# Block sums of the values from a copy of their own, and value tiles loaded in three pieces without the summary rows

## The chip, the core and the metric

The kernel runs on one core of a Trainium2 chip. The metric is the device time of one execution in microseconds (us); a figure for a kernel is the median of several executions. A profile is one more execution, recorded by the hardware; its span runs from the core's first instruction to its last. The engines are named TensorE (PE in rows, PEld its weight loads), VectorE (DVE), ScalarE (ACT), GpSimd (POOL) and SyncE (SP, which issues the DMA transfers).

## What is computed

Inputs are q, k and v of 4 batches, 8 heads, 768 positions and 64 columns, the routing matrix phi (512 x 32), and w1 and w2 of 8 experts. All is float32.

```python
k_sum = k.reshape(B, H, nb, block, D).max(axis=3)      # blocks of 32 positions, nb = 24
v_sum = v.reshape(B, H, nb, block, D).mean(axis=3)
scores_l = scale * q @ k.T      # kept where |i - j| < 16
scores_s = scale * q @ k_sum.T + log(block)
a = softmax(concatenate([scores_l masked, scores_s]))
x = a @ concatenate([v, v_sum])
# then a soft mixture of experts on x as (3072, 512):
logits = x @ phi
slots = softmax over rows(logits).T @ x       # 32 slots, 4 an expert
slot_out[e] = relu(slots[e] @ w1[e]) @ w2[e]
out = softmax over slots(logits) @ slot_out
```

So each query sees its 31 neighbours and 24 block summaries, and every block needs the maximum of its keys and the sum of its values.

## The kernel before, in words

**Tiles.** Work is cut into eight groups `hb` of four heads of one batch, and each group into three steps `tp` of 256 queries: 24 steps, `i` = 3 `hb` + `tp`. Within a step `tt` tells two halves of 128 queries, and `ab` two windows of 64 queries in each half. A window needs 96 positions (`W`) and 24 summaries (`NB`), together `U` = 120 rows. A value tile `v` is 128 partitions by 1040 columns: for both `ab`, both `tt` and four heads 64 columns and a one. It is laid out on the host; neighbouring windows overlap, so half of the positions stand there twice. Rows 96 to 119 of window `ab` = 0 and rows 32 to 55 of `ab` = 1 (`S0`) are left for the summaries; the load brings zeros and ones there, and `put_v` (L231) overwrites them.

**One step** (the loop at L522): `scores(i)` on TensorE (L253), `soft_max` (VectorE L271, GpSimd L275), `soft_exp` on ScalarE (L280), and for the step before, `j = i - 1`, transposes (`trans`, L286), their copies (`evac`, L291), `values` (L309) and a step later still `norm` (L329). TensorE's order is the order of the code.

**Summaries.** `k_max` (L184) takes block maxima of the next group's keys on VectorE in steps with `i % 3` = 1 and 2. `v_sum` (L200), called V(m) for group m, has four parts: 12 matmuls with an indicator matrix that add up blocks in the three value tiles of the group (L208); a copy on ScalarE and a difference on VectorE that split the sums into two parts (L219, L220), in a tile `vp`; two matmuls with a selection matrix (L224) that bring the 24 rows to their place; and a copy to `vsst` (L229). From there `put_v` writes them into the value tiles of the group. The four column groups of the array each take 32 output rows, so four of the 12 matmuls can run side by side.

**Where pieces stand.** `PLAN` (L42) lists for a step which parts of V, and of the routing (X a transposed x tile, L logits, t and D the slot sums), come where: text ahead of the bar before `soft_exp(i, 0)`, text behind it just before `values(j)`, the second string behind `values`. Each naming advances a piece by one part. V(m) begins in step 3m.

**Loads.** SyncE issues all loads in the order of the code: keys `k` (two of 472 KB a group), queries `q` (512 KB for two steps), value tiles (520 KB a step, requested four steps ahead into five buffers), and weights (512 KB each, 64 in all). `LOADS` (L39) says how many weights are requested at the end of each step; 36 in all, and 28 by the end of step 19. Eight semaphores take turns, so a load also waits until the one eight places before it has landed. A load into a buffer waits for the last reader of what was in it, and everything behind it on SyncE waits too.

**Behind the loop** come the last routing pieces (`TAIL`), a softmax over the slots, and the two expert stages with the rest of the weights (L651, L684) and the output (L711, L722).

Of the kernel before, what the change touches and what calls it, by code (L numbers as in the profile page):

```python
# [80 lines left out]
def attention_soft_moe(  # L81
# [48 lines left out]
    order = ["wa"] * NWA + "vp kp kp vp xs qp vp vp kp kp vp xs xs xs xs".split()  # L130
    NPRE = len(order)

    def load_piece():
# [4 lines left out]
        pool = {"wa": wa, "kp": kp, "qp": qp, "vp": vp_, "xs": xs}[slot[k]]
        t = pool.tile([128, 1024], F32, name=f"w{k}", tag=slot[k])
        p = pieces[k]  # L140
        if p[0] == "w1":
            _, e, c = p
            nc.sync.dma_start(out=t, in_=w1[e, 128 * c : 128 * c + 128, :])
        else:
            nc.sync.dma_start(out=t, in_=w2[p[1]])
# [19 lines left out]
    def load_v(i):  # L165
        if i < NSTEP:
            hb, tp = steps[i]
            v = vp_.tile([128, VC], F32, name=f"v{i}", tag="vp")
            nc.sync.dma_start(out=v, in_=vx[hb, tp])
# [30 lines left out]
    def v_sum(hb):  # L200
        pv = post_bank()
        for tp in range(TPS):
            v = vt[hb * TPS + tp]
            for tt in range(2):
                for ab in range(2):
                    g = tt * 2 + ab
                    ic = C_IND + 36 * ab + 4 - 2 * tp
                    nc.tensor.matmul(  # L208
                        pv[32 * g : 32 * g + 32, 0:256],
                        lhsT=cs[0:U, ic : ic + 32],  # L210
                        rhs=v[0:U, ab, tt, :, 0:64],
                        start=(tp == 0),
                        stop=(tp == TPS - 1),
                        tile_position=(0, 32 * g),
                    )
# [203 lines left out]
    def lanes():  # L419
# [317 lines left out]
def _layout(q, k, v):  # L737
# [22 lines left out]
    return kx.reshape(HB, 2, 128, KROW), np.ascontiguousarray(qx), vx.reshape(HB, TPS, 128, VC)  # L760


def _constants():
# [11 lines left out]
    ind = np.zeros((128, 2, 36), np.float32)  # L775
    for ab in range(2):
        for n in range(64):
            ind[16 + n + (NB if 16 + n >= S0[ab] else 0), ab, 4 + n // 32] = 1.0
    cst[:, C_IND : C_IND + 72] = ind.reshape(128, 72)
# [37 lines left out]
```

## Time and profile before

| | |
|---|---|
| median of three executions | 194.6 us (194.44 to 195.55) |
| the profiled execution | 193.69 us |
| its span | 191.9 us, granted TensorE clock 0.982 |
| TensorE busy | 170.6 us (89%) |
| VectorE, ScalarE, GpSimd busy | 114.7, 92.1, 78.7 us |
| bytes moved | 67.64 MB, mean 352 GB/s |
| first step's scores begin; step 21 begins | 7.96 us; 112.72 us |
| first expert matmul | 140.37 us |

A row of a timeline gives start, duration, engine, line, operation, what is written and read, a count, and in brackets how long the engine stood idle ahead of it and what ended that. A row of windows gives for a stretch the busy time of each engine, with the number of its instructions, the granted clock, the share of the transfer engines' time (it can pass 1 by a little) and what they moved. In rows of waits stand the total, the number and the longest.

### The profile page before, as it was taken

Reading aid. Unit: us, or ns where it says so; the run is one execution under the profiler, and the core shown is the slowest. Engines: PE = TensorE matmul, PEld = TensorE weight load, DVE = VectorE, ACT = ScalarE, POOL = GpSimd, SP = SyncE. Lnnn points to the kernel's source line nnn. Section 1 sums busy time; section 2 is a strip of 40 time slices with the busy share of each in tenths; the row PEclk is TensorE's granted clock in tenths of the full one; section 3 lists DMA queues with packets and bytes.
Section 4 is the critical chain, followed back from the end, with each engine's and each line's share of the span. In section 5 each row is a group of like instructions: output and inputs, shape, how many; then the busy total and the mean of one; then the engine's idle time right before and its main releaser. Section 6 shows DMA issues by size and latency. Waiting matters only on the chain.

```text
span 191.9 us, 7827 instructions
## 1 busy us (share of the span) xinstructions
PE 170.6 (89%) x3163; PEld 128.6 (67%) x3163; DVE 114.7 (60%) x580; ACT 92.1 (48%) x202; POOL 78.7 (41%) x106
## 2 busy tenths in 40 slices
PE   6979899799699999799999999998899998889950
PEld 5637678668567768578868786977456677667720
DVE  2539959649547967977967867755685020153460
ACT  2035656657464766756585484775222030033440
POOL 2047766666644685576684465780010000000000
PEclk9999999999999999999999999999969999999996
DMA  6999999999999899999999965967689999987696
GB/s 206 348 416 416 419 413 423 411 419 419 396 417 365 256 378 416 403 404 334 314 360 406 352 258 207 359 224 289 235 317 325 416 421 416 415 340 281 252 402 254
DMA packets 19331, 67.64 MB, mean 352 GB/s; under 512 B 2144, under 2 KB 2528, under 8 KB 19296
## 3 DMA queue, kind: packets, MB, share of 16 engines
q1 hardware_dynamic: 19296, 67.15, 90.2%
q8 instruction: 25, 0.41, 0.8%
q14 instruction: 10, 0.08, 0.1%
HBM read 60.85 MB, written 6.29 MB: 350 GB/s over the span
## 4 chain that ended last, share of the span: by engine, by line
PE 61%; DVE 14%; issue 7%; ACT 5%; DMA 4%; POOL 4%; SPq 2%; POOLq 0%; ACTq 0%; DVEq 0%
PE o L309 9%; PE hps L651 8%; PE so L684 8%; PE pt L286 7%; PE s L253 7%; PE pp L208 6%; DVE p L271 5%; DMA v<-vx 4%; PE op L711 4%; DVE kh L184 4%; POOL p L275 3%; PE pp L356 3%; PE pp L399 2%; PE pp L340 2%; DVE x L329 2%
## 5 line engine op out<-in xcount | busy, mean ns | idle before, releaser
L275 POOL TENSOR_TENSOR p<-p,m 128x480 f32<-128x480 f32 x48 | 46.4, 986 | 23.6 <-DVE m L271 23.3
L271 DVE CUSTOM_DVE_ANT_0 p<-s,cs 128x120 f32<-128x120 f32 x192 | 41.0, 278 | 5.7 <-PE s L253 4.7
L280 ACT ACTIVATE p<-p 128x480 f32<-128x480 f32 x48 | 29.0, 608 | 21.9 <-POOL p L275 21.6
L235 POOL COPY v<-vsst 24x520 f32<-24x520 f32 x47 | 29.1, 620 | 19.9 <-issue 17.6
L291 ACT COPY ptr<-pt 120x512 f32<-120x512 f32 x48 | 26.5, 588 | 21.3 <-PE pt L286 20.8
L309 PEld LDWEIGHTS o<-v,ptr 120*64 120x64 f32 x736 | 24.2, 137 | 10.0 <-issue 4.6
L309 PE MATMUL o<-v,ptr 120*64 120x65 f32 x736 | 27.7, 225 | 1.9 <-issue 1.5
L286 PE MATMUL pt<-ident,p 128*120 128x128 f32 x192 | 27.3, 281 | 0.8 <-ACT p L280 0.7
L253 PE MATMUL s<-k,q 64*64 64x120 f32 x768 | 26.2, 269 | 1.2 <-DVE m L271 0.6
L286 PEld LDWEIGHTS pt<-ident,p 128*120 128x120 f32 x192 | 20.4, 138 | 5.7 <-issue 2.8
L253 PEld LDWEIGHTS s<-k,q 64*64 64x64 f32 x768 | 20.4, 133 | 5.4 <-issue 2.5
L184 DVE TENSOR_REDUCE kh<-k 128x30 f32<-128x480 f32 (+1 forms) x32 | 16.1, 545 | 2.9 <-DMA k<-kx 2.9
L329 DVE TENSOR_TENSOR x<-o,z 128x512 f32<-128x512 f32 x23 | 15.9, 692 | 0.8
L271 DVE DVE_READ_ACCUMULATOR2_ANT m<- 128x1 f32 x192 | 16.0, 83 | 0.0
L651 PE MATMUL hps<-w,W1ST 128*32 128x256 f32 x256 | 15.7, 411 | 0.0
L720 DVE COPY ot<-op 128x512 f32<-128x512 f32 x12 | 7.9, 687 | 11.6 <-PE op L711 11.6
L684 PE MATMUL so<-w,W1ST 128*32 128x128 f32 x256 | 13.4, 275 | 0.9 <-issue 0.9
L208 PE MATMUL pp<-v,cs 120*32 120x256 f32 x192 | 12.4, 384 | 1.8 <-DMA v<-vx 1.0
L651 PEld LDWEIGHTS hps<-w,W1ST 128*32 128x32 f32 x256 | 8.9, 119 | 6.5 <-issue 1.8
L684 PE MATMUL so<-w,W2ST 128*32 128x128 f32 x256 | 13.1, 273 | 0.0
L340 PE MATMUL pp<-ident,x 128*128 128x128 f32 x88 | 12.5, 274 | 0.3 <-ACT xt L346 0.3
L346 ACT COPY xt<-pp 128x512 f32<-128x512 f32 x21 | 12.0, 602 | 0.1
(112 smaller groups left out, 180.2 us busy)
## 6 DMA issues: line engine op xcount, KB each, us to landing
w<-w SPq DMA_DIRECT2D x64, 512.0 KB, 8.1
v<-vx SPq DMA_DIRECT2D x24, 520.0 KB, 7.3
k<-kx SPq DMA_DIRECT2D x16, 472.0 KB, 7.2
q<-qx SPq DMA_DIRECT2D x12, 512.0 KB, 6.8
out<-ot SPq DMA_DIRECT2D x10, 512.0 KB, 3.6
out<-ot SPq DMA_DIRECT2D x4, 256.0 KB, 3.4
cs<-cst SPq DMA_DIRECT2D x1, 288.0 KB, 6.5
self__116<-selx SPq DMA_DIRECT2D x1, 64.0 KB, 6.2
```

The costliest lines, as they stand in the source:

```text
L184: nc.vector.reduce_max(out=kh[:, pr, :, n0 : n0 + m], in_=v[:, :, c0 : c0 + 16 * m].rearrange("p j (m k) -> p j m k", k=16), axis=AX,)
L208: nc.tensor.matmul(pv[32 * g : 32 * g + 32, 0:256], lhsT=cs[0:U, ic : ic + 32], rhs=v[0:U, ab, tt, :, 0:64], start=(tp == 0), stop=(tp == ...
L235: eng.tensor_copy(out=v, in_=src)
L253: nc.tensor.matmul(ps_[i, ab][h : h + 64, u, :], lhsT=qt[i // 2][rows, c : c + 64], rhs=kt[hb, pr][rows, k0 : k0 + U], start=True, stop=Tr ...
L271: nc.vector.tensor_tensor_reduce(out=p[:, n, :], in0=ps_[i, ab][:, 2 * tt + pr, :], in1=maskv[:, mk, :], scale=-0.125, scalar=-NEG, op0=AL ...
L275: nc.gpsimd.tensor_tensor(out=p, in0=p, in1=m.unsqueeze(2).broadcast_to([128, 4, U]), op=ALU.subtract)
L280: nc.scalar.activation(out=p, in_=p, func=AF.Exp, scale=-1.0)
L286: nc.tensor.transpose(pt[:, n, :], p[:, n, :], ident)
L291: nc.scalar.copy(out=ptr, in_=ptr_[i, tt])
L309: nc.tensor.matmul(o[64 * ab : 64 * ab + 64, h, :], lhsT=ptr[:, 2 * pr + ab, 64 * (r ^ ab) : 64 * (r ^ ab) + 64], rhs=v[0:U, ab, tt, h, :] ...
L651: nc.tensor.matmul(hps[32 * j : 32 * j + 32, :], lhsT=W1ST[:, c, 28 * e : 28 * e + 32], rhs=t[:, j, :], start=(k == 0), stop=(k == 31), ti ...
L684: nc.tensor.matmul(so[32 * j : 32 * j + 32, :], lhsT=W2ST[i][:, j, 28 * e : 28 * e + 32], rhs=t[:, i, j, :], start=(e == 0 and i == 0), st ...
```

## The change

`v_sum` reads an input of its own, `vox`: for each group all six tiles of 128 positions by four heads of 64 columns, each position once, 128 partitions by 1536 columns (768 KB). Six matmuls do what 12 did: tiles 0 to 3 in the four column groups, tiles 4 and 5 once more in the first two; the indicator and selection matrices change to match. `load_vo(hb)` requests it: group 0 right behind the selection matrix and ahead of the first value tiles, group 1 at the start as well (as two loads in two buffers of the pool for x tiles), and group m + 1 at the end of step 3m. The copy has a single buffer, `vo`, and V's split sums `vp` take the same buffer when the matmuls have read it.

A value tile is loaded in three pieces that leave out the rows for the summaries: rows 0 to 31 whole (4160 bytes each), rows 32 to 95 of the first half of the columns and rows 56 to 119 of the second half (2080 bytes each). The host packs the input to match (`_rows`). There are four value buffers, not five, and a tile is requested three steps ahead.

`PLAN` puts the first half of V(m) into step 3m - 1 for m from 1 on and the second half into step 3m (V7 has both in step 20), and shifts route pieces. `LOADS` asks for no weights in steps 0 to 2 and for more later. Two small tiles of the tail move to another buffer, since `vp` is no longer in their pool.

```diff
-LOADS = [1, 1, 1, 2, 2, 1, 2, 1, 2, 1, 1, 2, 2, 1, 1, 1, 1, 2, 1, 2, 3, 2, 2, 1]
+LOADS = [0, 0, 0, 1, 1, 2, 2, 1, 2, 1, 2, 2, 1, 2, 1, 2, 2, 2, 2, 2, 2, 3, 2, 1]
 PLAN = {
     0: ("V0 | V0", ""),
-    3: ("V1 | V1", "V1 V1"),
-    5: ("X0 X0 X1 X1", ""),
-    6: ("X2 X2 V2 | V2", "V2 V2"),
-    7: ("X3 X3", ""),
-    8: ("L0 | L0", ""),
-    9: ("t0 t0 X4 X4 V3 | V3", "V3 V3 D0 D0"),
+    2: ("V1 | V1", ""),
+    3: ("V1 V1", ""),
+    5: ("X0 X0 V2 | V2", ""),
+    6: ("V2 V2 X1 X1", ""),
+    7: ("X2 X2 X3 X3", ""),
+    8: ("L0 V3 | L0 V3", ""),
+    9: ("V3 V3 t0 t0", "D0 D0"),
...
-    20: ("X15 X15", "L3 L3"),
-    21: ("t3 t3 V7 | L3 V7 D3 D3", "V7 V7"),
-    22: ("X16 X16 X17 X17", ""),
+    20: ("X15 X15 V7 | V7", "V7 V7 L3 L3"),
+    21: ("t3 t3 X16 X16 | L3", "D3 D3"),
+    22: ("X17 X17", ""),
 }
-    vp_ = ctx.enter_context(tc.tile_pool(name="vp_", bufs=5))
+    vp_ = ctx.enter_context(tc.tile_pool(name="vp_", bufs=4))
+    vo = ctx.enter_context(tc.tile_pool(name="vo", bufs=1))
 def load_v(i):
-            nc.sync.dma_start(out=v, in_=vx[hb, tp])
+            n = S0[1]
+            nc.sync.dma_start(out=v[0:n], in_=vx[hb, tp, 0 : n * VC].rearrange("(p c) -> p c", p=n))
+            for ab in range(2):
+                p0, c0, o = (n, S0[1] + NB)[ab], VC // 2 * ab, n * VC + ab * 64 * VC // 2
+                nc.sync.dma_start(
+                    out=v[p0 : p0 + 64, c0 : c0 + VC // 2],
+                    in_=vx[hb, tp, o : o + 64 * VC // 2].rearrange("(p c) -> p c", p=64),
+                )
+    def load_vo(hb):
+        if hb == 1:
+            halves = [xs.tile([128, 1024], F32, name=f"vo1{n}", tag="xs")[:, 0:768] for n in range(2)]
+        elif hb < HB:
+            whole = vo.tile([128, 1536], F32, name=f"vo{hb}", tag="vo")
+            halves = [whole[:, 0:768], whole[:, 768:1536]]
+            nc.sync.dma_start(out=whole, in_=vox[hb])
...
 def v_sum(hb):
-        for tp in range(TPS):
-            v = vt[hb * TPS + tp]
-            for tt in range(2):
-                for ab in range(2):
-                    g = tt * 2 + ab
-                    ic = C_IND + 36 * ab + 4 - 2 * tp
-                    nc.tensor.matmul(
-                        pv[32 * g : 32 * g + 32, 0:256],
-                        lhsT=cs[0:U, ic : ic + 32],
-                        rhs=v[0:U, ab, tt, :, 0:64],
...
+        for t in range(6):
+            g = t % 4
+            ic = C_IND + 4 - 4 * (t // 4)
+            nc.tensor.matmul(
+                pv[32 * g : 32 * g + 32, 0:256],
+                lhsT=cs[:, ic : ic + 32],
+                rhs=kst["vo", hb][t],
+                start=(t < 4),
+                stop=(t + 4 > 5),
+                tile_position=(0, 32 * g),
+            )
-        vp = wk.tile([128, 2, 256], F32R, name="vp", bufs=1)
+        vp = vo.tile([128, 2, 256], F32R, name="vp", tag="vo")
 # start
-    for i in range(TPS):
-        load_v(i)
+    load_vo(0)
+    load_v(0)
+    load_v(1)
+    load_q(1)
+    load_k(1)
+    load_vo(1)
+    load_v(2)
+    load_v(3)
     nc.sync.dma_start(out=phi_sb.rearrange("p c s -> p (c s)"), in_=phi)
-    load_k(1)
-    load_q(1)
-    load_v(3)
-    load_v(4)
 # end of step i
+        if i > 0 and i % TPS == 0:
+            load_vo(i // TPS + 1)
         for _ in range(LOADS[i] if i < 20 else 0):
             load_piece()
         if i > 0:
-            load_v(i + 4)
+            load_v(i + 3)
```

The requests of SyncE at the start, behind the keys and queries of step 0; `self` is the selection matrix, and the numbers behind an underscore only tell buffers apart. Before:

```order
L506 DMA self__116<-selx 128x128
L169 DMA v_118<-vx 128x1040
L169 DMA v_120<-vx 128x1040
L169 DMA v_122<-vx 128x1040
L509 DMA phi_sb<-phi 128x128
L157 DMA k_125<-kx 128x944
L157 DMA k_127<-kx 128x944
L163 DMA q_129<-qx 128x1024
```

With the change:

```order
L527 DMA self__119<-selx 128x128
L189 DMA vo_121<-vox 128x1536
L173 DMA v_123<-vx 32x1040
L176 DMA v_123<-vx 64x520 x2
L173 DMA v_127<-vx 32x1040
L176 DMA v_127<-vx 64x520 x2
L166 DMA q_131<-qx 128x1024
L160 DMA k_133<-kx 128x944
L160 DMA k_135<-kx 128x944
L192 DMA vo_137<-vox 128x768
L192 DMA vo_138<-vox 128x768
```

V0 waited for the third value tile, and now waits for the first transfer behind the selection matrix; the next group's keys have the copy, two value tiles and q ahead of them.

TensorE at V7. Before, it stood in step 21, behind that step's scores (L253), transposes (L286) and the route piece t3 (L388):

```order
L286 MATMUL pt<-ident,p 120x128 x8
L388 MATMUL pp<-ident,dt 128x128
L208 MATMUL pp<-v_1875,cs 32x256 x4
L208 MATMUL pp<-v_1982,cs 32x256 x4
L208 MATMUL pp<-v_2086,cs 32x256 x4
L399 MATMUL pp<-x_1476,dsb 32x512 x2
L399 MATMUL pp<-x_1580,dsb 32x512 x2
L309 MATMUL o<-v_1764,ptr 64x65 x16
L224 MATMUL pp<-vp,sel 128x256 x2
```

With the change, in step 20, between the route transposes X15 (L361) and the values of step 19 (L330):

```order
L361 MATMUL pp<-ident,x_1591 128x128 x4
L229 MATMUL pp<-vo_2001,cs 32x256 x6
L330 MATMUL o<-v_1781,ptr 64x65 x16
L245 MATMUL pp<-vp,sel 128x256 x2
L377 MATMUL pp<-xt,phi_sb 32x128 x16
```

Twelve matmuls on three value tiles become six on one copy, and they stand one step earlier, ahead of the values of the step before.

The block sums' requests in the second half of the loop, from the end of step 17: the copy of group 7 stands behind the value tile of step 20 and ahead of step 18's weights.

```order
L160 DMA k_1896<-kx 128x944
L160 DMA k_1898<-kx 128x944
L146 DMA w_1900<-w 128x1024
L146 DMA w_1902<-w 128x1024
L173 DMA v_1904<-vx 32x1040
L176 DMA v_1904<-vx 64x520 x2
L189 DMA vo_2001<-vox 128x1536
L146 DMA w_2003<-w 128x1024
```

Before, V7 read the last of its three value tiles, which was requested at the end of step 19; its copy is now requested at the end of step 18.

More of the change, by code (lines that the diff above doesn't have):

```diff
@@ L35 @@
 C_N = 576
-LOADS = [1, 1, 1, 2, 2, 1, 2, 1, 2, 1, 1, 2, 2, 1, 1, 1, 1, 2, 1, 2, 3, 2, 2, 1]
+LOADS = [0, 0, 0, 1, 1, 2, 2, 1, 2, 1, 2, 2, 1, 2, 1, 2, 2, 2, 2, 2, 2, 3, 2, 1]
 PLAN = {
     0: ("V0 | V0", ""),
[19 rows of a table removed]
+    2: ("V1 | V1", ""),
[5 more added lines that the diff above has]
+    9: ("V3 V3 t0 t0", "D0 D0"),
+    10: ("X4 X4 X5 X5", ""),
+    11: ("X6 X6 V4 | V4", ""),
+    12: ("V4 V4 X7 X7", "L1 L1"),
+    13: ("t1 t1 X8 X8 | L1", ""),
+    14: ("D1 V5 | D1 V5", ""),
+    15: ("V5 V5 X9 X9", ""),
+    16: ("X10 X10 X11 X11", ""),
+    17: ("L2 V6 | L2 V6", ""),
+    18: ("V6 V6 t2 t2 | L2", "X12 X12 D2 D2"),
+    19: ("X13 X13 X14 X14", ""),
+    20: ("X15 X15 V7 | V7", "V7 V7 L3 L3"),
+    21: ("t3 t3 X16 X16 | L3", "D3 D3"),
+    22: ("X17 X17", ""),
     23: ("X18 X18", "x19 x19"),
@@ L86, in attention_soft_moe @@
     vx: bass.AP,
+    vox: bass.AP,
     phi: bass.AP,
@@ L128, in attention_soft_moe @@
     wt, slot = {}, {}
-    order = ["wa"] * NWA + "vp kp kp vp xs qp vp vp kp kp vp xs xs xs xs".split()
+    order = ["wa"] * NWA + "kp kp vp xs vo qp vp vp kp kp vp xs xs xs xs".split()
     NPRE = len(order)
@@ L137, in load_piece @@
         slot[k] = slot[k - NPRE] if k >= NPRE else order[k]
-        pool = {"wa": wa, "kp": kp, "qp": qp, "vp": vp_, "xs": xs}[slot[k]]
+        pool = {"wa": wa, "kp": kp, "qp": qp, "vp": vp_, "vo": vo, "xs": xs}[slot[k]]
         t = pool.tile([128, 1024], F32, name=f"w{k}", tag=slot[k])
@@ L168, in load_v @@
             v = vp_.tile([128, VC], F32, name=f"v{i}", tag="vp")
-            nc.sync.dma_start(out=v, in_=vx[hb, tp])
-            vt[i] = v.rearrange("p (a t h c) -> p a t h c", a=2, t=2, h=4)
+            n = S0[1]
[6 more added lines that the diff above has]
+                )
+            vt[i] = v.rearrange("p (a t h c) -> p a t h c", a=2, t=2, h=4)
+    def load_vo(hb):
[5 more added lines that the diff above has]
+            nc.sync.dma_start(out=whole, in_=vox[hb])
+        if hb == 1:
+            for n in range(2):
+                nc.sync.dma_start(out=halves[n], in_=vox[hb, :, 768 * n : 768 * n + 768])
+        if hb < HB:
+            kst["vo", hb] = [halves[t // 3][:, 256 * (t % 3) : 256 * (t % 3) + 256] for t in range(6)]
     kst = {}
@@ L423, in lanes @@
         yield
-        fg = wk.tile([1, 160], F32, name="fg", tag="vp", bufs=1)
+        fg = wk.tile([1, 160], F32, name="fg", tag="p", bufs=3)
         gm, f = fg[:, 128:160], fg[:, 0:128].rearrange("p (g s) -> p g s", g=4)
@@ L432, in lanes @@
         yield
-        R = wk.tile([128, 128], F32, name="R", tag="vp", bufs=1)
+        R = wk.tile([128, 128], F32, name="R", tag="p", bufs=3)
         nc.vector.tensor_scalar(out=R, in0=ps["stk"], scalar1=pc[:, 0:1], scalar2=None, op0=ALU.mult)
@@ L759, in _layout, with _rows @@
     qx = qx.reshape(HB * TPS // 2, 2, 128, 512).transpose(0, 2, 1, 3).reshape(HB * TPS // 2, 128, 1024)
-    return kx.reshape(HB, 2, 128, KROW), np.ascontiguousarray(qx), vx.reshape(HB, TPS, 128, VC)
+    return kx.reshape(HB, 2, 128, KROW), np.ascontiguousarray(qx), _rows(vx.reshape(HB, TPS, 128, 2, VC // 2))
+def _rows(vx):
+    n = S0[1]
+    parts = vx[:, :, :n], vx[:, :, n : n + 64, 0], vx[:, :, n + NB : n + NB + 64, 1]
+    return np.concatenate([p.reshape(HB, TPS, -1) for p in parts], axis=2)
 def _constants():
@@ L773, in _constants @@
     cst[:, C_MASK:C_IND] = mask.reshape(128, 4 * U)
[L775 to L779, printed above, removed]
+    cst[np.arange(128), C_IND + 4 + np.arange(128) // 32] = 1.0
     sel = np.zeros((128, 128), np.float32)
@@ L782, in _constants @@
         for n0 in VS:
-            sel[32 * (n // 2 % 4) + 2 * (n // 8) + n % 2, n0 + n] = 1.0
+            sel[32 * (n // 4 % 4) + 4 * (n // 16) + n % 4, n0 + n] = 1.0
     p = np.arange(128)
@@ L799 @@
         "vx": vx,
+        "vox": np.ascontiguousarray(
+            inputs["v"].reshape(HB, 4, 6, 128, D).transpose(0, 3, 2, 1, 4).reshape(HB, 128, 6 * 256)
+        ),
         "phi": np.ascontiguousarray(inputs["moe_phi"].reshape(4, 128, NS).transpose(1, 0, 2).reshape(128, 4 * NS)),
```

4 lines of the change are left out of this document (removed), and 9 rows, old and new, of the table PLAN.

## The prediction

> **What bounds the kernel now.** I read the page first: shares of the engines, then the chain of work that ended last.
>
> ```profile
> span 191.9 us, 7827 instructions
> PE 170.6 (89%) x3163; PEld 128.6 (67%) x3163; DVE 114.7 (60%) x580; ACT 92.1 (48%) x202; POOL 78.7 (41%) x106
> GB/s 206 348 416 416 419 413 423 411 419 419 396 417 365 256 378 416 403 404 334 314 360 406 352 258 207 359 224 289 235 317 325 416 421 416 415 340 281 252 402 254
> PE 61%; DVE 14%; issue 7%; ACT 5%; DMA 4%; POOL 4%; SPq 2%; POOLq 0%; ACTq 0%; DVEq 0%
> ```
>
> TensorE is the bound on average, but the transfers run close behind. So I cut the span into stages: up to the first work that needed summaries (13.3), two halves of the attention loop (to 112.7, where step 21 begins), its end with the routing, and the experts.
>
> ```profile
> core 0: us, PE busy (x) PEld busy (x) DVE busy (x) ACT busy (x) POOL busy (x), PEclk, DMA share, GB/s
> 0.00:13.30 13.30, 10.53 (x76) 6.93 (x76) 4.80 (x24) 1.89 (x2) 3.20 (x11) 1.00 0.84 315
> 13.30:62.40 49.10, 44.42 (x887) 35.19 (x887) 35.72 (x211) 29.84 (x64) 30.53 (x39) 1.00 1.02 410
> 62.40:112.70 50.30, 47.67 (x946) 37.53 (x937) 39.37 (x221) 33.37 (x76) 32.48 (x42) 1.00 0.96 357
> 112.70:140.30 27.60, 25.77 (x433) 19.59 (x432) 17.92 (x89) 15.09 (x39) 12.42 (x16) 1.00 0.73 268
> ```
>
> The reader is to see two things. In the loop TensorE is busy 44.42 of 49.10 us and 47.67 of 50.30: work taken off it is time gained. And the transfers are saturated (410 GB/s) in the first half, with little room in the second; a change that moves more bytes must be checked against that. Behind 112.7 there is room again (268 of 410 GB/s).
>
> **TensorE's part.** On the chain one V piece reads so (third column: what, with its count), with the step's scores and transposes before it:
>
> ```profile
> 83.02 0.98 PE s L253 x32
> 84.00 1.02 PE pt L286 x8
> 85.02 1.43 PE pp L208 x24
> 86.45 0.71 PE o L309 x19
> ```
>
> Each matmul gives two records, so 24 records are the 12 matmuls of a V piece: three rounds of four, one per column group of the array, 1.43 / 3 = 0.48 us a round. The new piece has six matmuls: a full round and one that uses two groups of four. If a half-filled round costs a full one, 0.95 us remain and 0.48 is saved; if time follows the number of matmuls, 0.72 is saved. I take 0.48, because the two matmuls of a group must follow each other. The seven pieces V1 to V7 lie in the TensorE-bound loop: 7 x 0.48 = **3.4 us** (at most 7 x 0.72 = 5.0). The contraction grows from 120 to 128 rows; the columns that stream through, 256, stay, so I count nothing for it. V0 is counted with the start.
>
> **The moved halves.** The first half of V(m) moves from step 3m to step 3m-1 and route pieces move the other way. Steps 2, 5, 8, ... are those in which VectorE also takes block maxima. These are seven of them, each from its first scores matmul to the next step's:
>
> ```profile
> 17.37:21.66 4.29, 3.47 (x74) 2.81 (x73) 4.12 (x24) 2.77 (x6) 2.96 (x4) 1.00 1.02 416
> 30.81:36.07 5.26, 4.29 (x84) 3.75 (x81) 3.88 (x23) 3.87 (x9) 3.65 (x5) 1.00 1.03 416
> 45.27:51.42 6.15, 4.39 (x108) 3.63 (x105) 4.31 (x24) 3.67 (x11) 4.43 (x6) 1.00 1.02 400
> 61.91:66.63 4.72, 4.35 (x85) 3.67 (x81) 4.62 (x25) 3.73 (x8) 3.11 (x5) 1.00 0.85 258
> 76.90:82.95 6.05, 5.02 (x93) 3.73 (x89) 5.14 (x25) 4.33 (x10) 3.90 (x6) 1.00 1.01 406
> 91.45:95.99 4.54, 4.37 (x109) 3.69 (x105) 4.38 (x25) 2.48 (x7) 2.93 (x5) 1.00 0.92 310
> 107.73:112.72 4.99, 4.99 (x112) 4.15 (x109) 3.25 (x21) 2.78 (x7) 2.19 (x4) 1.00 0.83 319
> sum 36.00, PE 30.87 PEld 25.43 DVE 29.71 ACT 23.64 POOL 23.16; mean PE 4.41 PEld 3.63 DVE 4.24 ACT 3.38 POOL 3.31
> ```
>
> TensorE idles 36.00 - 30.87 = 5.1 us there, and VectorE is nearly full in the first, fourth and sixth. Work put into these steps can lie beside what already makes TensorE wait. At worst nothing is hidden (0), at best all 5.1. I take **1.5 us**: some of the idle time stands behind the V piece's new place and isn't reached by it.
>
> **The start.** V0 now needs the first three value tiles. The rows are the arrival of the selection matrix, the last round of V0, the scores of step 1, and the first block maxima of the next keys:
>
> ```profile
> 8.85 0.29 POOL L517 CAST sel<-self__116 128x128 fp32r<-128x128 f32 x1 [7.26 <-DMA self__116<-selx]
> 12.75 0.16 PEld L208 LDWEIGHTS pp<-v,cs 120*32 120x32 f32 x8 [1.18 <-DMA v<-vx]
> 13.32 0.43 PE L253 MATMUL s<-k,q 64*64 64x120 f32 x8
> 16.61 1.57 DVE L184 TENSOR_REDUCE kh<-k 128x30 f32<-128x480 f32 x3
> ```
>
> Right behind the selection matrix the new order requests the copy, 786 KB, which at 410 GB/s lands at 8.8 + 1.9 = 10.7; six matmuls of 0.95 end at 11.6, and the scores of step 1 begin 1.7 us earlier. But then come v0, v1, q1 (0.97, 0.97 and 1.28 us at that rate) and both halves of the next keys (2.36): 16.3, where the maxima, 1.7 us earlier, would want them whole by about 16.0. V1's copy, two loads of 393 KB, lands at 18.2, wanted when step 2's transposes are done: 17.37 - 1.7 + 2.0 = 17.7. I count **1.0 us** of gain; the bounds are 0.4 (1.3 us of it are lost again) and 1.7.
>
> **Bytes.** The copy is 8 x 786 KB = 6.29 MB more. A value tile without the 24 overwritten rows of each half is 399 instead of 532 KB: 24 x 133 = 3.19 MB less. Net 3.1 MB more, 7.6 us at 410 GB/s, all before step 21. Is it in the way? The copy for V(m) must land before TensorE reaches V(m). I add the bytes requested ahead of it in the new order (keys, queries, values, copies, weights), take the first 13.3 us at 315 GB/s (4.19 MB) and the rest at 410, and set against it the place where V(m) would stand at today's pace (step's start, 2.0 us for scores and transposes, and the route pieces ahead):
> - V2: 10.2 MB, 27.9 us; place 33.2
> - V3: 15.7 MB, 41.5; place 48.3
> - V5: 28.5 MB, 72.5; place 80.0
> - V7: 41.2 MB, 103.5; place 110.2
>
> So the queue allows a gain of 5.3 us early and 6.6 late. The last place is read here (scores, transposes, route transposes, and the values matmuls ahead of which V7 will stand):
>
> ```profile
> 107.73 1.05 PE L253 MATMUL s<-k,q 64*64 64x120 f32 x32
> 108.71 1.09 PE L286 MATMUL pt<-ident,p 128*120 128x128 f32 x8
> 109.63 0.60 PE L340 MATMUL pp<-ident,x 128*128 128x128 f32 x4
> 110.16 1.35 PE L309 MATMUL o<-v,ptr 120*64 120x65 f32 x32
> ```
>
> Fewer weights in steps 0 to 4 make the early room; 28 pieces are requested by the end of step 19 in both, and what follows has the room behind 112.7, so the experts' stage is counted unchanged.
>
> **Requests.** SyncE issues three loads a value tile instead of one, 57 requests more in all (48 and nine for the copies).
>
> ```profile
> 3.06 1.56 SPq L169 DMA_DIRECT2D v<-vx  x3
> SPq L169 <- PE o L309: 48.8, 18, 4.7
> SPq L145 <- DMA w<-w: 10.4, 11, 2.0
> w<-w SPq DMA_DIRECT2D x64, 512.0 KB, 8.1
> v<-vx SPq DMA_DIRECT2D x24, 520.0 KB, 7.3
> ```
>
> One issue costs 1.56 / 3 = 0.52 us, so 30 us of SyncE; it waits 48.8 us for the values matmuls to release value buffers, which covers this. Two costs stay. A load waits until the one eight places before it has landed (the third row is such a wait): eight loads with six small ones among them hold 1.8 MB rather than 4.1, so the queue can run dry. And the copy shares its buffer with V's intermediate, so its request waits for V(m-1)'s second matmul, two steps (about 9 us at the new pace) before its use, while loads take 7 to 8 us to land; behind this wait stand the weights and the next value tile, which has three more steps. Bounds for both: nothing, as the landing times fit, and 4 us, half a microsecond or so at each V piece. I take **0.9 us** lost, mostly at V1 and V2.
>
> **Sum.** 1.0 + 3.4 + 1.5 - 0.9 = 5.0 us less. The profiled execution took 193.7 (span 191.9 and 1.8 around it); the median shown is 194.6. So 194.6 - 5.0 = **189.6 us**, own range 187 to 192.5 from the terms' bounds.
>
> **Rivals.** *Pieces of a tile move slowly (slower).* Every load of the trace fills all 128 partitions; the new value loads fill 32 or 64. No row prices that. If the first and the last piece (133 KB each, 0.32 us at 410 GB/s) run at half the rate, a tile costs 0.65 us more, 21 tiles by V7 13.7: its copy lands at 117.2, 7.0 behind today's place; with the 0.5 us that V7 itself saves, 6.5 slower: 201. It decides from about 0.31 us a tile, that is when three pieces take as long as the whole tile does today (1.30 us): then the 6.6 us of room are gone. Against it: two pieces of different rows may be in flight at once and share. The lower bound of this cost is nothing.
> [...]
>
> *VectorE keeps the step (no change).* In three of the seven steps VectorE was busy 4.1 of 4.3, 4.6 of 4.7 and 4.4 of 4.5 us. If its chain of scores, maxima and normalisation sets every step, TensorE's savings become idle time and only the start's 1.0 remains: 193.6. Against it: TensorE is the fuller engine in both halves of the loop.
>
> *The copy isn't early (no change).* Should the request wait for the second matmul cost each of V2 to V7 0.8 us, 4.8 are lost and the gain is gone: 194.4. For it: loads land 7 to 8 us after issue in a window of 9; against it: the queue holds fewer bytes now, so they land sooner.
>
> **How the numbers follow.** The forecast gets 0.62 (with 0.05 for a gain over 7.6 us, where idle time is filled better), no change through VectorE 0.10, through late copies 0.08, slow pieces 0.20. One per cent, 1.9 us, is about what a measurement here can tell from none (three runs spread by 1.1). So faster 0.62, same 0.18, slower 0.20. The range runs from 187.0, where all but the largest gains lie, over the no-change cases to 197.0, which takes in slow pieces up to a third of the loss worked out.
>
> **What would show it.** Right: V pieces of 12 records near 0.95 us, none preceded by a wait for the copy over half a microsecond, step 20 starting about 4 us earlier, idle time of steps 2, 5, 8 smaller. Wrong: value loads whose packets keep the transfer engines longer than their bytes ask for, or waits of TensorE for `vo` that grow from V3 to V7: then the slow pieces hold. Steps unchanged with more idle TensorE: VectorE.

## The result, and the profile after

The changed kernel takes 218.3 us (median of four executions, 216.54 to 223.65), the kernel before 194.7 on the same chip: a ratio of 1.123 [1.116, 1.130], 12% slower, where 189.6 us was forecast. (Medians are of all executions of a kernel, but ratios leave out those more than 1.5% above its fastest; the experiment `mid` below has for that reason one execution left and no interval.)

These are rows of the page of the kernel after: span, engines, bandwidth by slices, packets, and the shares of the chain of work that ended last.

```profile
span 215.2 us, 7788 instructions
PE 174.6 (81%) x3067; PEld 132.3 (61%) x3067; DVE 114.5 (53%) x580; ACT 92.6 (43%) x202; POOL 78.6 (37%) x106
...
GB/s 205 353 314 322 225 296 361 279 400 338 308 308 317 351 302 401 322 329 300 312 375 294 370 303 325 304 263 400 386 191 354 244 405 416 419 415 404 338 293 302
DMA packets 22163, 70.73 MB, mean 329 GB/s; under 512 B 3056, under 2 KB 3440, under 8 KB 22128
...
PE 52%; DMA 34%; issue 3%; SPq 3%; DVE 2%; POOL 1%; ACT 1%; POOLq 0%; ACTq 0%
```

The chain has turned from 4% DMA to 34%. The bytes are what was planned (70.73 MB, 3.09 more than before), but the slices in the first three quarters read about 320 GB/s; before, the first half of the loop read 410 and the second 357. The last quarter, which loads weights and no values, again has slices over 400.

The same stages as before, by windows of the kernel after (step 1 begins at 12.47, step 21 at 137.75):

```profile
0.00:12.47 12.47, 9.69 (x64) 6.92 (x64) 4.81 (x24) 1.89 (x2) 3.20 (x11) 1.00 0.85 275
12.47:66.39 53.92, 45.98 (x832) 36.91 (x830) 35.93 (x210) 29.73 (x64) 30.46 (x39) 0.87 1.02 321
66.39:137.75 71.36, 52.04 (x934) 40.78 (x931) 39.48 (x222) 34.77 (x78) 33.60 (x43) 0.90 1.03 328
137.75:163.60 25.85, 23.48 (x404) 17.92 (x400) 16.78 (x84) 14.27 (x36) 10.42 (x13) 1.00 0.91 316
163.60:215.20 51.60, 43.46 (x847) 29.79 (x846) 17.55 (x41) 11.95 (x23) 0.95 (x1) 0.94 0.91 357
```

In the loop the transfer engines are busy all the time (1.02 and 1.03), yet move 321 and 328 GB/s. So the queue did not run dry; each byte took longer. Step 21 starts 25.0 us later than before, the first expert matmul also 25.0 later (165.37 against 140.37), and the span ends 23.3 later: the whole loss is made in the loop.

Within the loop it sits in one kind of step, the seven with V(1) to V(7) (steps 2, 5, ... 20, the same class as in the prediction). Three of them and the sum, by windows of the kernel after:

```profile
46.43:57.27 10.84, 6.87 (x120) 4.96 (x116) 4.65 (x25) 4.35 (x12) 4.63 (x7) 0.74 1.04 327
103.78:113.29 9.51, 5.38 (x120) 4.05 (x116) 5.24 (x27) 4.53 (x13) 4.61 (x7) 1.00 1.03 337
123.42:137.75 14.33, 8.23 (x125) 6.07 (x123) 5.25 (x25) 4.52 (x10) 4.32 (x6) 0.76 1.03 317
...
sum 67.27, PE 42.79 PEld 30.38 DVE 34.99 ACT 30.17 POOL 32.43; mean PE 6.11 PEld 4.34 DVE 5.00 ACT 4.31 POOL 4.63
```

They took 36.00 us before and take 67.27 now: 31.3 us more, against a loss of 25.0 by step 21; the other steps got shorter. What TensorE waits for there stands in the waits of the kernel after:

```profile
PE pp L229 <- DMA vo<-vox: 23.7, 9, 6.1
```

and, in TensorE's timeline of step 20, where:

```profile
123.42 1.05 PE L274 MATMUL s<-k,q 64*64 64x120 f32 x32
124.41 1.09 PE L307 MATMUL pt<-ident,p 128*120 128x128 f32 x8
125.33 0.60 PE L361 MATMUL pp<-ident,x 128*128 128x128 f32 x4
132.03 1.92 PE L229 MATMUL pp<-vo,cs 128*32 128x256 f32 x12 [6.10 <-DMA vo<-vox]
133.88 2.00 PE L330 MATMUL o<-v,ptr 120*64 120x65 f32 x32
```

TensorE is done with scores and transposes at 125.9 and stands 6.1 us before V(7), whose copy is missing. The chain of the kernel after has these copies as its links (start, duration; here V2, V3, V5 and V7):

```profile
29.40 7.20 DMA vo<-vox
...
45.22 8.13 DMA vo<-vox
...
83.04 9.18 DMA vo<-vox
...
122.66 9.24 DMA vo<-vox
```

They land at 36.6, 53.4, 92.2 and 131.9; the prediction had them at 27.9, 41.5, 72.5 and 103.5. The error (8.7, 11.9, 19.7 and 28.4 us) grows with the number of value tiles moved, as it must if every tile costs too much. The waits themselves don't grow steadily: 0.77 us at V2, 3.97 at V3, 1.79 at V5 and 6.10 at V7.

**Theories.** *Rows* (A in the expectations): a load that fills only 32 or 64 neighbouring partitions is slow, so the three pieces of a value tile are. *Number of loads* (B): three small loads are slower than one whatever they fill, through SyncE's issues or the queue. *Bytes* (C): the copies' 6.3 MB are simply too many. Most of the experiments vary one of these at a time.

### The profile page after: what moved, and what is told of

It reads as the page before. It is cut to its first block, busy times and chain, and to the rows that moved or that the text cites. A ratio compares the mean times of both kernels' runs of the same rounds, so it can differ in the third digit from the quotient of the medians.

```text
span 215.2 us, 7788 instructions
## 1 busy us (share of the span) xinstructions
PE 174.6 (81%) x3067; PEld 132.3 (61%) x3067; DVE 114.5 (53%) x580; ACT 92.6 (43%) x202; POOL 78.6 (37%) x106
## 2 busy tenths in 40 slices
DMA packets 22163, 70.73 MB, mean 329 GB/s; under 512 B 3056, under 2 KB 3440, under 8 KB 22128
## 4 chain that ended last, share of the span: by engine, by line
PE 52%; DMA 34%; issue 3%; SPq 3%; DVE 2%; POOL 1%; ACT 1%; POOLq 0%; ACTq 0%
DMA vo<-vox 24%; PE o L330 8%; PE so L709 7%; PE hps L676 7%; PE s L274 6%; PE pt L307 6%; PE pp L229 4%; DMA v<-vx 4%; PE op L736 4%; DMA q<-qx 3%; DMA k<-kx 3%; PE pp L361 3%; PE pp L377 2%; PE pp L420 1%; SPq L173 1%
## 5 line engine op out<-in xcount | busy, mean ns | idle before, releaser
L330 PEld LDWEIGHTS o<-v,ptr 120*64 120x64 f32 x736 | 27.5, 153 | 10.5 <-issue 9.5
L330 PE MATMUL o<-v,ptr 120*64 120x65 f32 x736 | 31.2, 241 | 2.8 <-issue 2.4
L229 PE MATMUL pp<-vo,cs 128*32 128x256 f32 x96 | 11.8, 496 | 23.7 <-DMA vo<-vox 23.7
L274 PE MATMUL s<-k,q 64*64 64x120 f32 x768 | 28.2, 284 | 2.2 <-issue 1.8
L274 PEld LDWEIGHTS s<-k,q 64*64 64x64 f32 x768 | 22.0, 143 | 8.0 <-issue 5.8
L307 PEld LDWEIGHTS pt<-ident,p 128*120 128x120 f32 x192 | 20.9, 140 | 4.1 <-issue 3.0
L229 PEld LDWEIGHTS pp<-vo,cs 128*32 128x32 f32 x96 | 4.1, 127 | 28.7 <-issue 23.8
L241 DVE TENSOR_TENSOR vp<-pp,vp 128x256 fp32r<-128x256 f32 x8 | 3.4, 425 | 25.8 <-ACT vp L240 25.8
L676 PE MATMUL hps<-w,W1ST 128*32 128x256 f32 x256 | 15.2, 401 | 0.0
L709 PE MATMUL so<-w,W1ST 128*32 128x128 f32 x256 | 14.0, 275 | 1.2 <-issue 1.2
L361 PE MATMUL pp<-ident,x 128*128 128x128 f32 x88 | 12.9, 275 | 1.2 <-issue 0.9
```

Source lines behind the costliest of these rows:

```text
L229: nc.tensor.matmul(pv[32 * g : 32 * g + 32, 0:256], lhsT=cs[:, ic : ic + 32], rhs=kst["vo", hb][t], start=(t < 4), stop=(t + 4 > 5), tile_ ...
L274: nc.tensor.matmul(ps_[i, ab][h : h + 64, u, :], lhsT=qt[i // 2][rows, c : c + 64], rhs=kt[hb, pr][rows, k0 : k0 + U], start=True, stop=Tr ...
L307: nc.tensor.transpose(pt[:, n, :], p[:, n, :], ident)
L330: nc.tensor.matmul(o[64 * ab : 64 * ab + 64, h, :], lhsT=ptr[:, 2 * pr + ab, 64 * (r ^ ab) : 64 * (r ^ ab) + 64], rhs=v[0:U, ab, tt, h, :] ...
L361: nc.tensor.transpose(pv[:, 128 * c : 128 * c + 128], x, ident)
L676: nc.tensor.matmul(hps[32 * j : 32 * j + 32, :], lhsT=W1ST[:, c, 28 * e : 28 * e + 32], rhs=t[:, j, :], start=(k == 0), stop=(k == 31), ti ...
```

## Experiments

To compare transfer rates I use one window for all kernels, from 20 to 100 us, inside the loop. Its rows for the kernel before, and then for the kernel after:

```profile
20.00:100.00 80.00, 73.55 (x1461) 58.21 (x1461) 60.55 (x359) 51.42 (x115) 52.25 (x66) 1.00 0.99 385
```

```profile
20.00:100.00 80.00, 65.24 (x1168) 51.95 (x1172) 50.88 (x298) 42.48 (x93) 44.23 (x56) 0.87 1.02 321
```

385 GB/s before, 321 after, at a share of 0.99 and 1.02.

### 1. rows4, spread4, cols4: four loads a tile, cut in three ways

The kernel before, with each whole value tile loaded by four loads of 133 KB: 32 neighbouring partitions each, or every fourth partition, or 260 of 1040 columns of all partitions.

```diff
-            nc.sync.dma_start(out=v, in_=vx[hb, tp])
+            for n in range(4):
# rows4
+                nc.sync.dma_start(out=v[32 * n : 32 * n + 32], in_=vx[hb, tp, 32 * n : 32 * n + 32])
# spread4
+                nc.sync.dma_start(out=v[n:128:4], in_=vx[hb, tp, n:128:4])
# cols4
+                nc.sync.dma_start(out=v[:, 260 * n : 260 * n + 260], in_=vx[hb, tp, :, 260 * n : 260 * n + 260])
```

> The kernel before, with each value tile loaded as four loads of 32 neighbouring rows (133 KB each, 4160 bytes a row) in place of one; same bytes, nothing else changed. Theory A (a load that fills part of the partitions runs slowly, by which rows it fills): at half rate a tile costs 1.3 us more, 24 tiles 31 us; the loop's queue has some 7 us of room, so 212 to 222 us. Theory B (it is the number of loads and their size): slower too, and as much as the two kernels that cut the tile in another way. Theory C (only the copy's bytes slowed the changed kernel): within 1% of 194.7.

> The kernel before, with each value tile loaded as four loads of 32 rows again, but every fourth row (n, n + 4, n + 8, ...), so that each load is spread over all partitions; same bytes, same number and size of loads as with neighbouring rows. Theory A: 194 to 198 us, since each load reaches everything a whole tile reaches. Theory B: as slow as with neighbouring rows. Theory C: within 1% of 194.7.

> The kernel before, with each value tile loaded as four loads of 260 columns by all 128 rows (133 KB each, 1040 bytes a row). Theory A: 194 to 199 us, a little for shorter rows. Theory B: the slowest of the three, as its rows are shortest. Theory C: within 1% of 194.7.

| | us | ratio to before | GB/s, 20 to 100 us | transfer share |
|---|---|---|---|---|
| rows4 | 237.5 | 1.217 [1.205, 1.228] | 274 | 1.01 |
| spread4 | 204.1 | 1.049 [1.040, 1.058] | 360 | 0.99 |
| cols4 | 199.3 | 1.023 [1.016, 1.030] | 372 | 1.01 |

Same bytes, same number of loads, same load size: rows4 loses 22%, the others 5% and 2%. So neighbouring rows are what costs. Rows4 and spread4 lie well above what *Rows* expected (212 to 222 and 194 to 198 us), cols4 just above (194 to 199). The cut into more loads costs something too: with 72 loads more cols4 loses 4.5 us and spread4 9.6, some 0.06 and 0.13 us each (cols4 also has shorter rows, 1040 bytes for 4160). Why every fourth row is dearer than columns wasn't resolved.

### 2. halves and mid: fewer loads, other rows

Again the kernel before; `halves` has only 24 loads more than it, `mid` has 48.

```diff
-            nc.sync.dma_start(out=v, in_=vx[hb, tp])
# halves
+            for n in range(2):
+                nc.sync.dma_start(out=v[64 * n : 64 * n + 64], in_=vx[hb, tp, 64 * n : 64 * n + 64])
# mid
+            for n in (slice(0, 32), slice(32, 96), slice(96, 128)):
+                nc.sync.dma_start(out=v[n], in_=vx[hb, tp, n])
```

> The kernel before, with each value tile as two loads of 64 neighbouring rows (266 KB each). If it counts which rows a load fills, and rows 0 to 63 are served no better than 0 to 31: as slow as four loads of 32 neighbouring rows, 228 to 240 us. If a load of 64 rows has three quarters of the rate or so, 205 to 215. If it is the number of loads (24 more): 196 to 200.

> The kernel before, with each value tile as three loads of rows 0 to 31, 32 to 95 and 96 to 127 (133, 266 and 133 KB). If it counts which rows a load fills and the middle one, half of it in each half of the partitions, is served like a whole tile, half of the loss with four loads of 32 rows stays (237.5 - 194.9 = 42.6): 212 to 219 us. If any load of neighbouring rows below 128 is slow: 230 to 238. If it is the number of loads: 198 to 203.

`halves` took 241.1 us (240.1 to 245.61), 1.242 [1.230, 1.254], just above the 228 to 240 expected if rows count. The four executions of `mid` took 213.28, 217.32, 219.83 and 220.25 us, 1.10 to 1.13 times the kernel before; its profile is of the one at 219.83. The common window of halves, and then of mid:

```profile
20.00:100.00 80.00, 59.57 (x1038) 46.12 (x1041) 42.87 (x249) 36.17 (x80) 37.24 (x47) 0.86 1.03 277
```

```profile
20.00:100.00 80.00, 68.17 (x1245) 52.68 (x1244) 53.07 (x303) 44.18 (x95) 45.20 (x57) 0.94 1.03 318
```

Two loads a tile, of 64 rows each, are as slow as four of 32 (277 and 274 GB/s), so the number of loads falls as the main cause. With three loads, whose middle one takes rows 32 to 95, about half of the loss goes away (18.7 to 25.6 us of halves' 46.5 stay, by the fastest and the slowest execution): it matters which 64 rows. The reads from device memory are contiguous in rows4, halves and mid alike, so that side doesn't tell them apart. The transfer engines' share stays at 1.03. What makes rows 32 to 95 cheaper than rows 0 to 63 or 64 to 127 isn't shown by these runs.

The size is another matter. An estimate: in this window of halves, 23 loads of 266 KB are 6.1 of 22.1 MB, so values are 28% of the bytes. If all other loads ran at the 416 GB/s that `whole` (below) reaches, 1/277 = 0.72/416 + 0.28/x gives x = 149 GB/s for the halves, about a third of those 416 and not the half that the prediction's rival took. Part of that may be that other loads in the queue wait behind the slow ones; the runs don't separate it.

### 3. whole: the change with whole value tiles

The kernel after in all but the value loads: each tile is one load of 128 rows, the overwritten rows included, 3.2 MB more.

```diff
-            n = S0[1]
-            nc.sync.dma_start(out=v[0:n], in_=vx[hb, tp, 0 : n * VC].rearrange("(p c) -> p c", p=n))
...
+            nc.sync.dma_start(out=v, in_=vx[hb, tp])
```

> The changed kernel with one thing undone: a value tile is one load of 128 rows again (532 KB, with the rows that the summaries overwrite). 3.2 MB more are moved than in the changed kernel. Theory A: the queue moves 410 GB/s again, V7's copy lands near 111 us, and the time falls to 193 to 199 us. Theory B: likewise faster, by the 48 loads fewer. Theory C: slower than the changed kernel, 3.2 MB at its 325 GB/s being 10 us: 225 us or more.

It took 194.5 us, a ratio of 1.000 [0.995, 1.005] (the profiled execution 196.6). The pieces cost 218.3 - 194.5 = 23.8 us, net of the 3.2 MB that they save: the whole loss. The common window of whole:

```profile
20.00:100.00 80.00, 70.15 (x1389) 56.53 (x1387) 58.91 (x351) 50.37 (x111) 51.10 (x65) 0.98 1.02 416
```

The rate is 416 GB/s, nothing left. But the forecast gain doesn't appear either, and the waits and the last copy of whole (from its chain) say why:

```profile
PE pp L222 <- DMA vo<-vox: 13.1, 7, 3.8
```

```profile
101.26 11.31 DMA vo<-vox
```

V(7)'s copy lands at 112.6. The prediction's way of adding bytes, with 24 rows of each half put back in (44.0 MB ahead of it), gives 13.3 + (44.0 - 4.19) / 0.410 = 110.4, against a place of 110.2. So at full rate that method holds to 2.2 us, and it says that whole tiles and the copies together use up all the room.

### 4. thirds: the pieces' bytes and number, on all rows

The kernel after with three loads a tile of 260 columns by 128 partitions: 399 KB in three loads, as in the change.

```diff
+            for n in range(3):
+                nc.sync.dma_start(out=v[:, 260 * n : 260 * n + 260], in_=vx[hb, tp, :, 260 * n : 260 * n + 260])
...
-                    rhs=v[0:U, ab, tt, h, :],
+                    rhs=v[0:U, ab, tt * (1 - ab), h, :],
```

> The changed kernel with a value tile's three loads cut by columns instead of rows: 260 columns by all 128 rows each, 399 KB in sum as in the changed kernel, the same number of loads in the same places. The last quarter of a tile isn't loaded, and the values matmuls that need it take the quarter before; so those outputs are left out, at the same work. Theory A (which rows a load fills): the cost of the pieces goes, V7's copy lands near 104 to 108 us and the time is 188 to 195. Theory B (three small loads a tile are slow however cut): 214 to 221, as the changed kernel.

It took 195.6 us, 1.003 [0.998, 1.008], just above the 188 to 195 that *Rows* expected. The common window of thirds:

```profile
20.00:100.00 80.00, 71.07 (x1389) 57.94 (x1387) 59.11 (x346) 49.26 (x109) 50.50 (x64) 0.98 1.02 387
```

Bytes (70.73 MB), number of loads and order are those of the change; only the rows that a load fills differ (and with them the length of a row, 1040 bytes for 4160 and 2080), and 22.7 of the 23.6 us are gone. This is the cleanest proof of *Rows*. It also shows that leaving out bytes in small loads buys nothing here: 3.2 MB less than `whole`, but 387 instead of 416 GB/s.

### 5. one_copy: whole tiles, with next to no copies

`whole` with half of group 0's copy loaded once, and every V fed from it; V's split sums get a buffer of their own. The sums of the other groups are left out.

```diff
-            whole = vo.tile([128, 1536], F32, name=f"vo{hb}", tag="vo")
...
+            half = vo.tile([128, 1024], F32, name="vo0", tag="vo")[:, 0:768]
+            nc.sync.dma_start(out=half, in_=vox[0, :, 0:768])
+            for n in range(HB):
+                kst["vo", n] = [half[:, 256 * (t % 3) : 256 * (t % 3) + 256] for t in range(6)]
...
-        vp = vo.tile([128, 2, 256], F32R, name="vp", tag="vo")
+        vp = wk.tile([128, 2, 256], F32R, name="vp", bufs=1)
```

> The changed kernel with value tiles as one load again and with the copy of group 0 alone: half of it (393 KB) is loaded once at the start, and every V piece sums the same three tiles of 128 positions twice. The sums of the groups are left out, so only the order and amount of work count: six matmuls a V piece and the new places, without the copies' 5.9 MB. Theory A with the TensorE terms of the prediction (1.0 + 3.4 + 1.5 us): 188.8, between 187 and 191.5 us. Theory that the terms were too large, since other engines keep the steps: 193 to 195.

It took 183.3 us, 0.946 [0.937, 0.955], beyond the lower end of 187 that was expected. One V piece in its timeline, and the group of all eight:

```profile
30.34 1.06 PE L216 MATMUL pp<-vo,cs 128*32 128x256 f32 x12
```

```profile
L216 PE MATMUL pp<-vo,cs 128*32 128x256 f32 x96 | 8.4, 384 | 0.0
```

So with the copies out of the way TensorE's saving is real: no idle time before V, and 1.06 us a piece where the same view of the kernel before has 1.50. Of 11.3 us, 8.2 are made by the start of step 23 (114.44 against 122.60). That is more than the 5.9 us of the prediction's three gains. Fewer bytes aren't the reason, since this kernel moves 68.0 MB and the one before 67.6. Requesting no weights in steps 0 to 2 may be part of it (experiment 8 finds a gain of that kind); the rest wasn't taken apart.

### 6. late_w: weights out of the loop

The copies' bytes must give way to something. `late_w` is `whole` with 20 instead of 28 weights requested by the end of step 19, 4.2 MB less in the loop.

```diff
-LOADS = [0, 0, 0, 1, 1, 2, 2, 1, 2, 1, 2, 2, 1, 2, 1, 2, 2, 2, 2, 2, 2, 3, 2, 1]
+LOADS = [0, 0, 0, 0, 1, 1, 1, 1, 1, 1, 1, 1, 1, 1, 1, 1, 2, 2, 2, 2, 4, 5, 4, 3]
```

> The changed kernel with value tiles as one load again, and with 20 weights instead of 28 requested by the end of step 19 (36 by the end of the loop as before); nothing else. If the copies' bytes ahead of V7 are what took the gain, 4.2 MB less there are 10 us of transfers: V pieces stop waiting and the time is 188 to 192 us. Theory that the weights then come late for the experts, as the room behind step 21 is 3.9 MB: 194 us or more, with waits for weights at the expert matmuls.

It took 190.9 us, 0.985 [0.977, 0.993]. In the profiled executions step 21 starts at 106.82 instead of 118.58 in `whole`, 11.8 us earlier, but the span ends only 5.8 earlier (189.0 against 194.8), and the medians are 3.6 apart. VectorE's timeline of late_w shows a loss behind the loop:

```profile
135.60 0.29 DVE L448 TENSOR_SCALAR R<-stk,pp 128x128 f32<-128x128 f32 x1 [5.28 <-DMA stk<-selx]
```

The 64 KB matrix `stk`, requested behind the loop, now stands in line behind the late weights, and the softmax over the slots waits 5.3 us for it. Behind that wait TensorE's six records `pcl<-ident,lt_all` take 1.54 us on the chain; in the kernel before they take 0.88. Work moved back in the queue delayed what was requested after it.

### 7. early_stk and early_stk23: the small matrix ahead of the weights

The edits against late_w:

```diff
+        if i == 20:
+            ps["stk"] = const.tile([128, 128], F32, name="stk", tag="sel")
+            nc.sync.dma_start(out=ps["stk"], in_=selx[1])
         for _ in range(LOADS[i] if i >= 20 else 0):
             load_piece()
...
-    ps["stk"] = const.tile([128, 128], F32, name="stk", tag="sel")
-    nc.sync.dma_start(out=ps["stk"], in_=selx[1])
# early_stk23 also
-LOADS = [0, 0, 0, 0, 1, 1, 1, 1, 1, 1, 1, 1, 1, 1, 1, 1, 2, 2, 2, 2, 4, 5, 4, 3]
+LOADS = [0, 0, 0, 0, 1, 1, 1, 1, 1, 1, 1, 2, 1, 2, 1, 2, 2, 2, 2, 2, 3, 4, 4, 2]
```

> The kernel with whole value tiles and late weights (190.9 us), and the 64 KB matrix of the tail (selx[1]) requested at the end of step 20, ahead of the late weights rather than behind twelve of them. Its trace showed 5.3 us of VectorE waiting for that load, and TensorE at half clock behind it. If that wait is all that is left of the copies' cost: 184 to 186.5 us. If the weights are late themselves: 189 to 191.

> As the kernel before it, but 23 weights by the end of step 19 rather than 20. If the transfers ahead of V7 still bind with 23: 3 x 1.28 = 3.8 us later there, 187 to 190 us. If there is room: within 1 us of the kernel with 20.

`early_stk` took **186.1 us, 0.958 [0.954, 0.962]**: the best complete version, 4.2% faster than before. With 23 weights instead of 20 by step 19 it is 188.9 us, 0.967 [0.962, 0.972], within the 187 to 190 expected if the transfers ahead of V7 still bind; one execution of that kernel, the profiled one, took 834.5 us for a reason I don't know, so no row of it is used. Rows of early_stk: the page, then the waits, then the sum of the seven steps by windows.

```profile
span 184.5 us, 7693 instructions
...
DMA  6999999999999999999999999999999999999994
...
DMA packets 20627, 73.93 MB, mean 401 GB/s; under 512 B 2288, under 2 KB 2672, under 8 KB 20592
```

```profile
PE pp L222 <- DMA vo<-vox: 0.5, 2, 0.3
PEld pp L222 <- DMA vo<-vox: 1.2, 2, 0.8
```

```profile
sum 38.63, PE 35.80 PEld 26.19 DVE 30.10 ACT 25.72 POOL 26.11; mean PE 5.11 PEld 3.74 DVE 4.30 ACT 3.67 POOL 3.73
```

The wait for copies falls from 23.7 to 0.5 us on the matmuls (and from 4.3 to 1.2 on their weight loads), and the transfers are now busy from end to end at 401 GB/s. TensorE is 89% busy, so both stand near their bound; that three more weights in the loop cost 2.8 us says that bytes still count.

### 8. before_late: how much of it is not V's change

The control: the kernel before, with late_w's weights, and `stk` requested at the end of step 21.

> A control: the kernel before, with the two moves of the 186.1 us kernel alone, 20 weights by the end of step 19 instead of 28 and the tail's matrix requested in the loop (here at the end of step 21, where V7 is done). If that kernel's gain comes from the six matmuls, the earlier V0 and the new places, and late weights only make room for the copies: within 1% of the kernel before. If late weights are a gain of their own: 188 to 192 us.

It took 191.2 us, 0.983 [0.977, 0.990], within the range named for late weights being a gain of their own (188 to 192). So some 1.7%, 3.3 us, of early_stk's gain comes from the two moves by themselves. That gain is made by step 9, which starts at 47.62 instead of 51.42. Half of it lies in step 8, where TensorE of the kernel before stands idle in the middle of a logits piece:

```profile
49.98 0.42 PE L356 MATMUL pp<-xt,phi_sb 128*32 128x128 f32 x7 [1.76 <-issue]
```

With later weights this gap is gone, but the trace names nothing that it waited for ("issue"), so how early weights cause it stays open. V's change with whole tiles is then worth 0.958 / 0.983 = 0.974, some 5.0 us (3.6 to 6.6 by the two intervals).

## Why the prediction was wrong, point by point

**The step that failed is "Bytes".** It priced 41.2 MB ahead of V(7)'s copy at 410 GB/s, whatever a load fills, and so had the copy land at 103.5 with 6.6 us of room. It landed at 131.9. At full rate the step holds (`whole`: 110.4 by that way, 112.6 measured); with pieces it needs a price per tile. From the windows of after: from 12.47 to 137.75 us, 321 x 53.92 + 328 x 71.36 make 40.7 MB in 125.3 us; at 416 GB/s they take 97.9. The missing 27.4 us over some 22 tiles are about 1.25 us a tile (an estimate). 21 x 1.25 on top of 103.5 gives 129.8. What *Requests* costs is in these 1.25 us too.

**The rival held, and cost about twice a tile what it said.** "Pieces of a tile move slowly" named place, wait and sign (transfer engines kept busy longer than their bytes ask for, waits for `vo`, the longest at V7 though not growing at every step). It took half the rate for the first and last piece, 0.65 us a tile, and so 201 us. That half was an assumption which no run shows; the runs show some 1.25 us a tile (the estimate above) and 218.3. The argument I set against it, that two pieces of different rows may be in flight at once and share, is what `halves` speaks against: its two loads of a tile follow each other directly, between them fill all rows, and still move 277 GB/s. It was the only argument set against the rival, which got 0.20. The prediction itself had worked out that 0.31 us a tile decides, and had no row that held the cost below that.

**Requests.** The 0.9 us was probably too small as well. It isn't tested alone, but `thirds` against `whole` bounds it. By V7's copy thirds has 2.8 MB less to move, 6.7 us at 416 GB/s, yet V7 starts at 111.88 and 112.70, only 0.8 earlier. So the cut into three loads took some 6 us of transfers there, an estimate and an upper bound, because the rows of thirds are shorter too (1040 bytes). By cols4's 0.06 us a load, 57 loads make 3.4 us. In the changed kernel no copy's request waited for V's second matmul; those that waited did so mostly for loads ahead of them.

**TensorE's part was right in mechanism and about right in size.** Four column groups do run side by side: by the chain rows in the prediction, 24 V records of 256 columns pass in 1.43 us, 0.06 each, while the transposes' records of 128 columns, which use the groups together, take 1.02 / 8 = 0.13. The longer contraction cost nothing: a V record lasts 384 ns in the mean with 120 rows (kernel before) and with 128 (one_copy). A half-filled round does cost nearly a full one. In the view that gave 1.43 us for twelve matmuls, the chain, the six take 0.85 to 0.99 us in early_stk, and 0.95 was taken; timelines have 1.50 and 1.06. By these rows the seven pieces save 3.1 to 4.1 us, and 3.4 was taken.

**The start.** The prediction counted 1.0 us. Step 1 begins at 12.47 in the changed kernel (0.85 earlier than 13.32) and at 11.77 in early_stk, 1.55 earlier; before_late, without V's change, has 12.63, so 0.86 of it is V's. From early_stk's timeline, V(0) and what follows:

```profile
10.78 1.06 PE L222 MATMUL pp<-vo,cs 128*32 128x256 f32 x12 [0.19 <-DMA vo<-vox]
11.77 1.05 PE L267 MATMUL s<-k,q 64*64 64x120 f32 x32
```

In early_stk the copy landed about when it was worked out (10.7); in the changed kernel V(0) began at 11.49, after a wait of 1.00 us for it.

**The moved halves.** In early_stk the seven steps hold 35.80 - 30.87 = 4.9 us more TensorE work and take 38.63 - 36.00 = 2.6 us longer: 2.3 us less than the added work, where 1.5 was taken. But this doesn't show that the moved work hides: in before_late the same steps take 32.66 us with 30.27 of TensorE work, so against it 5.5 us more work cost 6.0 us more time. The 2.3 us may be the later weights' alone.

**The sum.** With copies that arrive, V's change is worth about 5.0 us (0.974), the size of the forecast. That the two agree is in part luck: it is another kernel, with whole tiles and later weights, and the term for moved work isn't confirmed. As the change is made, it comes with loads that cost 23.8. *VectorE keeps the step* is refuted by one_copy. *The copy isn't early* came true in `whole`, but mostly through bytes: three of its requests waited 3.5 us in total for V's second matmul, while the transfers were full (1.02) and V's matmuls waited 13.1. In early_stk four requests wait 5.6 us for that matmul and the copies still arrive in time. That `whole` lands on this rival's 194.4 us is luck.

## What to carry to other kernels

Where transfers are near their bound, price a load by the partitions it fills, not by its bytes alone: leaving out a quarter of a tile by rows made it slower than the whole tile (by the estimate above 0.96 + 1.25 = 2.2 us, against 1.28 for 532 KB at 416 GB/s). Cut a tile along its columns (cols4 lost 2% where rows4 lost 22%), or not at all, and count each extra small load as well (some 0.06 us in cols4). Before adding bytes to a full queue, look for what can be requested later, then look at what stands behind that in the queue: here the later weights were worth having even without the change, and a 64 KB matrix behind them made VectorE wait 5.3 us.

## What the runs showed of the hardware

**Loads of few neighbouring rows slowed the whole queue.** With every transfer engine shown busy (shares of 1.01 to 1.03) the total rate was 274 GB/s (32 neighbouring rows), 277 (64: lower and upper half), 318 (32, the middle 64, 32), and 416 for whole tiles. The 416 are from the changed kernel with its copies; the kernel before, with whole tiles, read 410 where its transfers were busy all the time.

**TensorE at half clock behind long waits.** In step 20 above, after 6.1 us without work, V's 12 records took 1.92 us and the values 2.00. In step 17 of the kernel after the wait was shorter:

```profile
111.22 1.06 PE L229 MATMUL pp<-vo,cs 128*32 128x256 f32 x12 [2.81 <-DMA vo<-vox]
112.21 1.15 PE L330 MATMUL o<-v,ptr 120*64 120x65 f32 x32
```

The same work took 1.06 and 1.15 us after 2.81 us; step 8, after 3.97 us, has 1.92 and 2.00 again. The windows of these steps show it as a granted clock of 0.74 (step 8) and 0.76 (step 20) beside 1.00 (step 17). Over V and the values alone the granted clock of the kernel after is 0.50 behind the waits of 3.97, 4.71 and 6.10 us (V3, V4 and V7) and 1.00 behind those of 1.79 and 2.81 (V5 and V6); these are the windows of V7 and V6:

```profile
132.03:135.88 3.85, 3.85 (x45) 2.51 (x45) 0.43 (x1) 0.88 (x2) 0.00 (x0) 0.50 1.03 278
111.22:113.29 2.07, 2.07 (x44) 1.46 (x44) 0.43 (x1) 0.88 (x2) 0.18 (x1) 1.00 1.03 305
```

The length of one wait isn't all, though. In step 2 two shorter waits, with six of V's records between them, were followed by the half clock (0.50 from 22.98 to 24.91):

```profile
20.52 0.71 PE L229 MATMUL pp<-vo,cs 128*32 128x256 f32 x6 [1.78 <-DMA vo<-vox]
21.97 1.08 PE L229 MATMUL pp<-vo,cs 128*32 128x256 f32 x6 [0.74 <-DMA vo<-vox]
22.98 2.00 PE L330 MATMUL o<-v,ptr 120*64 120x65 f32 x32
```

In the seven steps TensorE is busy 42.79 us for what takes it 35.80 in early_stk. Most of these 7.0 us are probably hidden, since TensorE goes on to wait for the next copy; behind V7, the last one, nothing hides them, and there V and the values take 1.7 us more than at full clock. So TensorE, which waited for data, also worked more slowly once it had arrived.
